# A hand-scheduled attention and state-space kernel: new durations and delays in the planner's model, a new seed and rules, and an earlier release of score banks

## The chip, the cores and the metric

The kernel runs on one core of one Trainium2 chip. The metric is the device time of one execution in microseconds (us), as the median of several. Engines are called by the names of the profile: PE is TensorE (matmuls), DVE is VectorE, ACT is ScalarE, POOL is GpSimd, SP is SyncE, which issues most DMAs.

## The reference, cut to what matters

Two independent layers on sequences of 2048 rows and 640 columns; their outputs stand side by side.

```python
# A: a diagonal state-space layer
Lam_bar = exp(dt * Lam);  B_bar = ((Lam_bar - 1) / Lam)[:, None] * Bmat
Bu = einsum("bld,pd->blp", x + 0j, B_bar)
for t in range(L):
    h = Lam_bar[None, :] * h + Bu[:, t, :]
y = 2.0 * einsum("blp,dp->bld", hseq, Cmat).real + x * Dskip
# B: attention, 32 query heads of width 20, one shared key and value head
q = (x @ wq).reshape(B, S, 32, 20);  k = x @ wk;  v = x @ wv
p = softmax(einsum("bhqd,bkd->bhqk", q, k) * 20 ** -0.5)
o = einsum("bhqk,bkd->bhqd", p, v).reshape(B, S, 640) @ wo
out = concatenate([y, o], axis=-1)
```

## The kernel before, in words

**The work.** The scores are 2048 tiles of 128 keys by 512 queries: 4 blocks of queries, 8 groups of four heads, 16 chunks of keys, 4 heads. A *block* in the code (`b`, 32 of them) is one group of heads for one block of queries, 64 tiles. Each tile needs a score matmul, an exponential, and a product with V.

**Two ways to make an exponential.** Most tiles go to ACT: a *fill* (`fill`, L1482) is one PE step that writes two or three score tiles into the banks of one of two PSUM slots (SC0, SC1, three banks each), and one ACTIVATE (L1519) turns them into probabilities (`PR`), 1024 or 1536 columns wide. The two slots alternate. The other tiles, *D tiles*, go to DVE (`fill_d`, L1717): it evicts the scores as int16 (L864, `BIG<-SC` or `BIG<-MB`), which reads as a piecewise-linear power of two in bfloat16; three shifted copies of that are made by DVE (L864, `BIG<-BIG`, one tile or two at a time) or POOL (L1834, two at a time) in `copy` (L1820), and the four versions are weighted in the product with V. An ACT tile takes one matmul with V (`MB<-PR,VP`), a D tile takes four (`MB<-BIG,VS`). A D tile is often the third tile of a fill, with only the first two going to ACT. `SHARE` limits how many of the tiles are D tiles, `LAST` and `POOL_LAST` how late they and POOL's copies may come.

**PE's two modes.** In *row mode* (S) up to four matmuls of 32 rows each run side by side; the scores use it. In *column mode* (C) four matmuls of 32 columns each do; the products with V and nearly all other products use it. Going from one to the other costs time (`SWITCH` in the planner).

**The other work.** Projections, the state-space layer (units, Y products, scans on DVE) and the output products are tasks with due times counted in score tiles (`background`, `unit_due`, `C_DUE`, `CB_FROM`, `O_STEP`, `Y_STEP`). Their matmuls go in column mode between fills, or as *riders*: `board` (L810) puts one piece of such a product on the row of the array that a fill leaves free. A step may consist of several pieces. The first goes ahead of the score matmuls and the rest behind them; the step then signals twice, once at the last score and once at its end (`op.twice`).

```python
            fns = [self.piece(r, *m, x) for m in step[0]]
            if len(fns) > 1:
                op.twice = len(op.fns)
            op.fns[:] = fns[:1] + op.fns + fns[1:]
```

`keep_source` adds filler matmuls (`MB<-KT,VZ`) when PE had little to do lately.

**What sets the order.** `planned` (L547) runs a simulation of the engines (`Schedule`) when the kernel is built. Each step has a duration, reads and writes; `seen` (L109) says when another engine sees its end, `ready` and `pick` choose the next step of an engine by priority, slack and rules, and `rules` (L1435) changes the rules with the number of tiles done (`STAGES`, L1444). `SEEDS` spreads the due times of tasks at random. `Emitter.plan` (L272) then turns the order into five fixed instruction streams with semaphore waits. On the chip nothing is chosen any more: each engine goes through its stream and waits where it must. A reader of a PSUM bank waits for the last step that wrote to it.

Of the kernel before, what the change touches and what calls it, by code (L numbers as in the profile page):

```python
# [24 lines left out]
class Op:  # L25
# [3 lines left out]
                 "seq", "land", "dma_key", "idx", "tail", "mode", "load", "late", "port", "after", "due", "table", "psum", "twice", "fence", "lands", "clear")  # L29

    def __init__(self, eng, fns, dur, deps=(), prio=5, reads=(), writes=(), prev=None, gate=None, hook=None,
# [7 lines left out]
        self.port, self.after, self.due, self.table, self.twice, self.fence, self.lands = port, [], None, None, None, None, None  # L39
# [6 lines left out]
class Schedule:  # L46
# [10 lines left out]
    SWITCH, STAY = 97.0, 1.2  # L57
# [66 lines left out]
    def ready(self, op):  # L124
# [3 lines left out]
        for d in op.deps:  # L128
            if d.end is None:
                return None  # L130
            v = self.seen(d, op.eng)
            if v > r:
                r = v
        return r

    def begin(self, op, eng):
# [32 lines left out]
        for lag in (0.0, 60.0, 100.0, 110.0, 115.0, 130.0, 150.0, 200.0):  # L169
# [92 lines left out]
class Emitter:  # L262
# [9 lines left out]
    def plan(self):  # L272
# [6 lines left out]
        needed = set()  # L279
        self.streams = {e: [] for e in Schedule.ENGINES}  # L280
        for op in self.order:
# [3 lines left out]
            def dep(o):  # L285
# [5 lines left out]
                if src not in need or need[src].idx < o.idx:  # L291
                    need[src] = o
# [3 lines left out]
            if op.fence is not None:  # L296
                need[e] = op.fence
# [6 lines left out]
            for k in op.reads:  # L304
                w = last_w.get(k)
                dep(w)
# [8 lines left out]
            if op.dma_key is not None:  # L315
                prev = dma_count.get(op.dma_key)
                if prev is not None:
                    need[op.dma_key] = prev[1]
            w = []
            K = know[e]  # L320
            items = sorted(need.items(), key=lambda kv: (kv[0] == e, -kv[1].start))
            for src, o in items:
                if K.get(src, -1) >= o.idx:
                    continue
                w.append(o)
# [3 lines left out]
                if K.get(src, -1) < o.idx:  # L329
                    K[src] = o.idx  # L330
            kept = []
            for o in w:
                src = o.dma_key if o.dma_key is not None else o.eng
                implied = False
                for o2 in w:
                    if o2 is not o and snap[id(o2)].get(src, -1) >= o.idx:
                        implied = True
                if not implied:
                    kept.append(o)
                    needed.add(id(o))  # L340
# [31 lines left out]
    def replay(self, rng):  # L372
# [3 lines left out]
        for op in self.order:  # L376
            e = op.eng
            t = free[e]
            for o in self.waits_of[id(op)]:
                lag = S.OUT["dma"] if o.dma_key is not None else S.OWN.get(e, 0.0) if o.eng == e else S.OUT[o.eng]  # L380
# [15 lines left out]
    def emit(self, block):  # L396
# [70 lines left out]
class Build:  # L467
# [77 lines left out]
    SEEDS, REPLAYS = (10005,), 12  # L545
# [264 lines left out]
    def board(self, op, used):  # L810
# [5 lines left out]
        for r in self.rides:  # L816
# [19 lines left out]
            if len(fns) > 1:  # L836
                op.twice = len(op.fns)
# [423 lines left out]
    def qt_task(self, bank, g=0):  # L1261
# [20 lines left out]
        if g:  # L1282
            ev = self.dve(lambda e: e.tensor_copy(dst, bank.ap), 645, deps=[prev], reads=[bank.key], writes=[key], prio=self.EV)
# [21 lines left out]
    def q_task(self, qb, blk, bank):  # L1305
# [6 lines left out]
        ev = self.dve(lambda e: e.tensor_copy(dst, bank.ap), 645, deps=[prev], reads=[bank.key], writes=[key], prio=self.EV)  # L1312
# [122 lines left out]
    def rules(self):  # L1435

        while self.stages and self.stages[0][0] <= self.tile_n:
# [12 lines left out]
        (250, {'ALONE': 2.237, 'PV': 1.984, 'COPY1': 0.897}),  # L1450
        (500, {'STAY': 1.083, 'SPARE': 86.026, 'SOON': 2941.52, 'ALONE': 2.429, 'TASK': 0.989, 'PV': 1.9, 'P1': 0.519, 'PVEV':
            0.2, 'SCARCE': 7, 'BACKLOG': 7, 'SHARE': 0.301}),
        (850, {'STAY': 1.2, 'dve': 185.73, 'MARGIN': 628.898, 'REFILL': 766.143, 'SPARE': 148.045, 'LAG': 240.378, 'SOON':
            2730.774, 'ALONE': 1.449, 'TASK': 0.95, 'PV': 1.889, 'EV': 0.544, 'P1': 0.5, 'SCARCE': 8, 'BACKLOG': 9}),
        (1200, {'STAY': 0.876, 'MARGIN': 648.138, 'REFILL': 905.623, 'LAG': 190.385, 'ALONE': 2.13, 'PV': 1.718, 'EV': 0.506,
            'COPY': 0.534, 'COPY1': 0.9}),
        (1600, {'STAY': 1.2, 'pe': 196.33, 'EARLIER': 5, 'ALONE': 1.525, 'PV': 1.9, 'COPY': 0.554, 'COPY1': 0.897, 'P1OWN': 0.321,
            'GRACE': 41.523}),
# [23 lines left out]
    def fill(self, op, i):  # L1482
# [28 lines left out]
        for m in extra:  # L1511
# [4 lines left out]
        op.dur = self.mmt(512, n_mm + (len(op.fns) > n_mm))  # L1516
# [3 lines left out]
                      0.8333 * 512 * n + 64, table="exp",  # L1520
# [196 lines left out]
    def fill_d(self, op, m, bank=None):  # L1717
# [12 lines left out]
        first = self.dve(self.ts(self.dr(h.index), bank.ap, 16256.0, 0.0, ALU.add, ALU.max), 645, deps=[op],  # L1730
# [61 lines left out]
    LAST = 16  # L1792
    POOL_LAST = 25
# [13 lines left out]
    POOL2 = 605.0  # L1807
# [43 lines left out]
    def pv_source(self):  # L1851
# [10 lines left out]
        scarce = len(self.d_free()) < self.SCARCE  # L1862
        for j in range(4):
# [752 lines left out]
```

## Time and profile before

| | us |
|---|---|
| runs of the kernel | 701.4, 702.19, 702.4 |
| median | 702.19 |
| the profiled execution | 701.32 |
| its span in the trace | 699.6 |

The profile is one execution. A row of the page gives a line, an engine, an operation, the tiles out<-in, their shape and count, then the busy time, the mean length of one in ns, and the idle time of that engine just before these instructions with what ended most of it. Rows of the timeline give the start, the time to the end of the last, the engine, line and operation, and how many were merged. Rows of windows give for each stretch the busy times of PE, weight loads, DVE, ACT and POOL with their counts, then PE's granted clock, the DMA share and GB/s. The chain of waits follows the work back from the last instruction. PE's granted clock is 1.00 throughout the main part.

### The profile page before, as it was taken

What the parts mean: (1) busy time and instruction counts of PE and PEld (TensorE: products, weight loads), DVE (VectorE), ACT (ScalarE), POOL (GpSimd) and SP (SyncE); (2) the same over time, 40 slices, a digit from 0 to 9 for tenths busy, and PEclk for the clock granted to TensorE, in tenths of its full rate; (3) what the DMA queues carried; (4) which work ended last, traced back from release to release, by engine and by line L of the source; (5) the groups of instructions that cost most, each with busy time, mean ns of one, the idle gap of its engine ahead of it and who ended that gap; (6) DMA issues with size and microseconds to landing.
All of it is one profiled execution on the core that took longest, in us unless ns stands there. A gap on an engine that the chain in (4) does not pass through costs nothing.

```text
span 699.6 us, 27005 instructions
## 1 busy us (share of the span) xinstructions
PE 685.1 (98%) x11348; PEld 248.6 (36%) x11350; DVE 629.7 (90%) x1211; ACT 685.3 (98%) x701; POOL 467.7 (67%) x796
## 2 busy tenths in 40 slices
PE   9999999999999999999999999999999999999997
PEld 5323232334333333534343323334333333343323
DVE  7899999999999987898979997899999999997695
ACT  7999999999999999999999999999999999999996
POOL 4266776443868898464777885777866777768780
PEclk9999999999999999999999999999999999999999
DMA  9649732001111111000040010131000011100001
GB/s 220 170 109 224 177 85 58 28 8 31 28 49 32 28 43 37 23 19 17 17 83 21 15 42 21 35 56 22 12 15 20 12 26 39 29 19 19 27 15 40
DMA packets 77590, 34.46 MB, mean 49 GB/s; under 512 B 58350, under 2 KB 77470, under 8 KB 77470
## 3 DMA queue, kind: packets, MB, share of 16 engines
q1 hardware_dynamic: 76506, 32.44, 19.0%
q8 instruction: 91, 1.49, 0.9%
q10 hardware_dynamic: 964, 0.29, 0.2%
q14 instruction: 29, 0.24, 0.1%
HBM read 11.53 MB, written 9.75 MB: 30 GB/s over the span
## 4 chain that ended last, share of the span: by engine, by line
PE 66%; ACT 33%; DVE 0%; issue 0%; DVEq 0%
ACT PR L1519 33%; PE MB L727 26%; PE MB L797 17%; PE SC L727 14%; PE MB L807 7%; PE SC L1155 1%; PE MB L723 1%; PE SC L723 0%; DVE PR L859 0%; PE MB L1272 0%; DVE mab L1161 0%; DVEq L510 0%; PE SC L1211 0%; DVE pvsb L859 0%; DVE M L863 0%
## 5 line engine op out<-in xcount | busy, mean ns | idle before, releaser
L1519 ACT ACTIVATE PR<-SC 128x1024 bf16<-128x1024 f32 (+1 forms) x677 | 670.3, 1171 | 3.9 <-PE SC L727 2.8
L1834 POOL INT64_ADD BIG<-BIG x761 | 455.4, 614 | 200.6 <-DVE BIG L864 72.3
L864 DVE TENSOR_SCALAR BIG<-SC 128x512 int16<-128x512 f32 x548 | 369.4, 684 | 49.8 <-PE SC L727 43.1
L727 PE MATMUL SC<-QT,KT 32*128 32x512 bf16 x2013 | 264.5, 384 | 6.9 <-ACT PR L1519 5.9
L727 PE MATMUL MB<-BIG,VS 128*32 128x512 bf16 x2332 | 257.4, 383 | 0.4 <-DVE pvsb L1901 0.2
L727 PE MATMUL MB<-PR,VP 128*32 128x512 bf16 x1465 | 213.7, 384 | 0.0
L727 PEld LDWEIGHTS SC<-QT,KT 32*128 32x128 bf16 x2013 | 66.7, 90 | 157.4 <-ACT PR L1519 94.7
L727 PEld LDWEIGHTS MB<-BIG,VS 128*32 128x32 bf16 x2332 | 61.7, 95 | 65.1 <-issue 40.6
L727 PEld LDWEIGHTS MB<-PR,VP 128*32 128x32 bf16 x1465 | 51.4, 94 | 44.6 <-issue 32.8
L797 PE MATMUL MB<-CT,W 128*32 128x320 bf16 (+2 forms) x996 | 52.7, 301 | 0.6 <-issue 0.6
L864 DVE TENSOR_SCALAR BIG<-BIG 128x1024 int16<-128x1024 int16 (+1 forms) x116 | 45.8, 427 | 1.5 <-PE MB L727 1.0
L807 PE MATMUL MB<-xaT,BT 32*128 32x256 bf16 x200 | 38.6, 272 | 0.7 <-ACT PR L1519 0.6
L797 PE MATMUL MB<-CA,W 128*32 128x512 bf16 (+1 forms) x640 | 35.4, 302 | 0.0
L797 PE MATMUL MB<-xaT,BA 128*32 128x256 bf16 x800 | 32.2, 275 | 0.0
L807 PE MATMUL MB<-diagD,xaT 32*128 32x128 bf16 x320 | 31.4, 217 | 0.0
L807 PEld LDWEIGHTS MB<-diagD,xaT 32*128 32x128 bf16 x320 | 17.7, 92 | 28.9 <-ACT PR L1519 20.2
L797 PEld LDWEIGHTS MB<-CT,W 128*32 128x32 bf16 x996 | 22.4, 96 | 15.3 <-issue 7.5
L2086 DVE CAST stg<-MB 128x512 bf16<-128x512 f32 x35 | 23.9, 683 | 1.9 <-PE MB L797 1.8
L797 PE MATMUL MB<-xaT,BT 128*32 128x256 bf16 x600 | 25.1, 274 | 0.0
L859 DVE TENSOR_TENSOR prod<-MB,tab 128x1024 bf16<-128x1024 f32 x20 | 24.3, 1216 | 0.4 <-PE MB L797 0.2
L864 DVE TENSOR_SCALAR BIG<-MB 128x512 int16<-128x512 f32 x35 | 23.8, 679 | 0.0
L2353 DVE TENSOR_TENSOR_SCAN g<-sc,hst,prod 128x256 bf16<-128x256 f32 x30 | 22.8, 772 | 0.1
(174 smaller groups left out, 488.1 us busy)
## 6 DMA issues: line engine op xcount, KB each, us to landing
out_dram<-stg SPq DMA_DIRECT2D x31, 128.0 KB, 1.8
qd<-BIG SPq DMA_DIRECT2D x20, 128.0 KB, 2.5
QT<-qd SPq DMA_DIRECT2D x28, 80.0 KB
OP<-pvsb SPq DMA_DIRECT2D x105, 20.0 KB
rdP<-recs SPq DMA_DIRECT2D x105, 20.0 KB
lbd<-BA SPq DMA_DIRECT2D x5, 320.0 KB, 4.1
CT<-in_B_x_dram SPq DMA_DIRECT2D x2, 640.0 KB, 5.3
BA<-in_A_B_re_dram SPq DMA_DIRECT2D x1, 800.0 KB, 9.4
```

Of the source, the lines that this page charges most:

```text
L723: r = e.matmul(out[32 * j:32 * j + 32], lhsT=lhsT[:, 32 * j:32 * j + 32], rhs=rhs, start=start, stop=stop, tile_position=(0, 32 * j), skip ...
L727: return lambda e: e.matmul(out, lhsT=lhsT, rhs=rhs, start=start, stop=stop, **kw)
L797: x = e.matmul(out[32 * j:32 * j + 32], lhsT=lhsT[:, 32 * j:32 * j + 32], rhs=rhs, start=start, stop=r.end is tag, tile_position=(0, 32 * ...
L807: return lambda e: e.matmul(out, lhsT=lhsT[at], rhs=rhs[at], start=False, stop=r.end is tag, tile_position=(32 * row, 0), skip_group_check ...
L859: return lambda e: e.tensor_tensor(out, a, b, op)
L864: return lambda e: e.tensor_scalar(out, a, s1, s2, op0=op0, op1=op1)
L1155: prev = self.pe([lambda e, x=x, c=c, n=n, at=at: e.matmul(bank.cols(n * x, n * x + n), lhsT=p.wks[:, 128 * c:128 * c + 128], rhs=p.xbT[:, ...
L1519: ex = self.act(lambda e: e.activation(dst, t[:, 0:512 * n], ACT.Exp, scale=1.0 / UNIT), 0.8333 * 512 * n + 64, table="exp", deps=[op], re ...
L1834: op.fns.append(lambda e: e.int64_add(words(dst), words(src), add))
L2086: ev = self.dve(lambda e: e.tensor_copy(st, bank.ap), 645, deps=[prev], reads=[bank.key], writes=[key], prio=self.EV, gate=(lambda: last.e ...
L2353: o = self.dve(lambda e, ri=ri, init=init: e.tensor_tensor_scan(p.g[:, u, ri, :], rdec, p.prod[:, 1, 0, ri, :], init, ALU.mult, ALU.add), ...
```

## The change

Three things are changed together. The edits of the model and of the rules touch only what the planner believes and prefers; the kernel gets other instruction streams through them.

1. *The model.* A change of PE's mode is taken as 105.5 ns and 10 more towards column mode; a change counts as starting when the results that the step reads are seen, not before. The delays between engines are set for each pair. A fill is one pass of 512 columns, whatever is in it. The exponential is 6 ns shorter, the evictions on DVE 7 ns, POOL's copy 18 ns.
2. *The rules.* A new seed, new values in all six stages, and new due times.
3. *The waits.* A reader of a PSUM bank that a step with riders wrote, where the bank is not the rider's own, waits for the step's first signal, that is the last score, and not for its end.

```diff
-    SWITCH, STAY = 97.0, 1.2
+    SWITCH, AFTER, STAY = 105.5, 10.0, 1.2
+    SEEN = {("pe", "act"): 225.0, ("pe", "dve"): 225.0, ("pe", "pool"): 285.0, ("act", "pe"): 92.0, ("dve", "pe"): 0.0, ("pool", "pe"): 0.0,
+            ("dve", "pool"): 170.0}
...
-        return op.end + self.OUT[op.eng]
+        return op.end + self.SEEN.get((op.eng, eng), self.OUT[op.eng])
...
             v = self.seen(d, op.eng)
+            if op.eng == "pe" and op.mode == self.mode and d.eng != "pe" and d.dma_key is None:
+                v += self.SWITCH
...
             if op.mode != self.mode:
-                op.dur += self.SWITCH
+                op.dur += self.SWITCH + (self.AFTER if op.mode == "C" else 0.0)
...
-            def dep(o):
+            def dep(o, key=None):
...
-                if src not in need or need[src].idx < o.idx:
-                    need[src] = o
+                at = o.idx - 0.5 if key is not None and o.twice is not None and key != o.rider else o.idx
+                if src not in need or need[src][0] < at:
+                    need[src] = at, o
...
             for k in op.reads:
-                w = last_w.get(k)
-                dep(w)
+                dep(last_w.get(k), k if k in self.psum else None)
...
+                if at < o.idx:
+                    self.first.add((id(op), id(o)))
...
-                        be.wait_ge(self.sems[o.eng], self.value[id(o)])
+                        be.wait_ge(self.sems[o.eng], self.value[id(o)] - ((id(op), id(o)) in self.first))
...
-    SEEDS, REPLAYS = (10005,), 12
+    SEEDS, REPLAYS = (750698,), 12
...
-                op.twice = len(op.fns)
+                op.twice, op.rider = len(op.fns), r.bank.key
...
     STAGES = (
-        (0, {'STAY': 1.2, 'PAUSE': 500.0, 'pe': 192.807, 'dve': 150.0, 'KEEP_C': 3, 'OPEN': 1, 'PATIENCE': 2500.0, 'MARGIN':
+        (0, {'STAY': 1.452, 'PAUSE': 500.0, 'pe': 192.807, 'dve': 150.0, 'KEEP_C': 3, 'OPEN': 1, 'PATIENCE': 2497.12, 'MARGIN':
...
-            7, 'AHEAD': 10, 'CAP': 3, 'ROOM': 4, 'ALONE': 1.397, 'TASK': 0.95, 'PV': 2.034, 'EV': 0.52, 'P1': 0.5, 'COPY': 0.554,
-            'COPY1': 0.836, 'P1OWN': 0.42, 'PVEV': 0.209, 'SCARCE': 8, 'BACKLOG': 9, 'GRACE': 55.439, 'SHARE': 0.29, 'MISC_FIRST':
+            7, 'AHEAD': 12, 'CAP': 2, 'ROOM': 4, 'ALONE': 1.397, 'TASK': 0.95, 'PV': 2.034, 'EV': 0.511, 'P1': 0.5, 'COPY': 0.554,
+            'COPY1': 0.836, 'P1OWN': 0.42, 'PVEV': 0.2, 'SCARCE': 8, 'BACKLOG': 9, 'GRACE': 55.439, 'SHARE': 0.29, 'MISC_FIRST':
...
-        op.dur = self.mmt(512, n_mm + (len(op.fns) > n_mm))
+        op.dur = self.mmt(512)
...
-                      0.8333 * 512 * n + 64, table="exp",
+                      0.8333 * 512 * n + 58, table="exp",
...
-    LAST = 16
-    POOL_LAST = 25
+    LAST = 8
+    POOL_LAST = 29
...
-    POOL2 = 605.0
+    POOL2 = 587.0
...
+        later = s.SWITCH if s.mode == "C" else 0.0
         for j in range(4):
-            can = [e for e in q[j] if e[4].end is not None and s.seen(e[4], "pe") <= t and self.vp_seen(e[1], t)]
+            can = [e for e in q[j] if e[4].end is not None and s.seen(e[4], "pe") <= t - later and self.vp_seen(e[1], t)]
...
-    C_DUE = 200
-    CB_FROM, CB_STEP = 358.689, 15.665
+    C_DUE = 103.686
+    CB_FROM, CB_STEP = 336.444, 15.665
...
-    Q_FROM, Q_STEP = (0, 30, 110, 190), 10.976
-    O_FROM, O_STEP, O_CLASS = 31.576, 38.293, 1
-    SSM_FROM, SSM_TO, Y_STEP, GRACE = 150.723, 1780, 23.0, 40
+    Q_FROM, Q_STEP = (0, 30, 110, 190), 11.747
+    O_FROM, O_STEP, O_CLASS = 31.576, 43.688, 1
+    SSM_FROM, SSM_TO, Y_STEP, GRACE = 150.723, 1780, 14.199, 40
```

The remaining lines of the diff set the evictions of DVE to 638 ns where they were 645, one product to 1144 for 1135, and the other five stages of the rules.

More of the change, by code (lines that the diff above doesn't have):

```diff
@@ L28 @@
     __slots__ = ("eng", "fns", "dur", "deps", "prio", "reads", "writes", "prev", "gate", "hook", "start", "end",
-                 "seq", "land", "dma_key", "idx", "tail", "mode", "load", "late", "port", "after", "due", "table", "psum", "twice", "fence", "lands", "clear")
+                 "seq", "land", "dma_key", "idx", "tail", "mode", "load", "late", "port", "after", "due", "table", "psum", "twice", "rider", "fence", "lands", "clear")
     def __init__(self, eng, fns, dur, deps=(), prio=5, reads=(), writes=(), prev=None, gate=None, hook=None,
@@ L38, in __init__ @@
         self.mode, self.load, self.late = mode, load, False
-        self.port, self.after, self.due, self.table, self.twice, self.fence, self.lands = port, [], None, None, None, None, None
+        self.port, self.after, self.due, self.table, self.fence, self.lands = port, [], None, None, None, None
+        self.twice = self.rider = None
         self.psum = any(k[0] == "B" and k[1:].isdigit() for k in self.reads)
@@ L168, in begin @@
         self.at(self.free[eng])
-        for lag in (0.0, 60.0, 100.0, 110.0, 115.0, 130.0, 150.0, 200.0):
+        for lag in (0.0, 60.0, 92.0, 100.0, 105.5, 110.0, 115.0, 130.0, 150.0, 170.0, 197.5, 225.0):
             self.at(op.end + lag)
@@ L279, in plan @@
         needed = set()
+        self.first = set()
         self.streams = {e: [] for e in Schedule.ENGINES}
@@ L296, in plan @@
             if op.fence is not None:
-                need[e] = op.fence
+                need[e] = op.fence.idx, op.fence
             for k in op.writes:
@@ L328, in plan @@
                         K[s2] = v
-                if K.get(src, -1) < o.idx:
-                    K[src] = o.idx
+                if K.get(src, -1) < at:
+                    K[src] = at
             kept = []
[L332 to L340, printed above, removed]
+            for src, at, o in w:
+                if any(o2 is not o and snap[id(o2)].get(src, -1) >= at for _, _, o2 in w):
+                    continue
+                kept.append(o)
+                needed.add(id(o))
+                if at < o.idx:
+                    self.first.add((id(op), id(o)))
             waits_of[id(op)] = kept
@@ L1450 @@
[L1450 to L1456, printed above, removed]
@@ L1874, in pv_source @@
         prio = 0.9 if tight or complete else self.PV
-        return Op("pe", [], self.mmt(512, len(group)), prio=prio, mode="C", load=128.0 * len(group), hook=lambda op: self.pv(op, b, group))
+        return Op("pe", [], self.mmt(512), prio=prio, mode="C", load=128.0 * len(group), hook=lambda op: self.pv(op, b, group))
     def vp_seen(self, kc, t):
```

39 lines of the change are left out of this document (25 added, 14 removed).

## The prediction

> **What bounds the kernel now.** I read the shares of busy time first, then the costliest groups split by shape, then who waited for whom.
>
> ```profile
> span 699.6 us, 27005 instructions
> PE 685.1 (98%) x11348; PEld 248.6 (36%) x11350; DVE 629.7 (90%) x1211; ACT 685.3 (98%) x701; POOL 467.7 (67%) x796
> L1519 ACT ACTIVATE PR<-SC 128x1024 bf16<-128x1024 f32 (+1 forms) x677 | 670.3, 1171 | 3.9 <-PE SC L727 2.8
> ```
> ```profile
> L1519 ACT ACTIVATE PR<-SC 128x1024 bf16<-128x1024 f32 x566 | 532.6, 1100 | 3.9 <-PE SC L727 2.8 <-PE MB L727 0.5
> L1519 ACT ACTIVATE PR<-SC 128x1536 bf16<-128x1536 f32 x111 | 159.9, 1534 | 0.0
> ```
> ```profile
> 200.00:300.00 100.00, 98.94 (x1767) 35.44 (x1759) 88.01 (x160) 100.00 (x104) 74.70 (x126) 1.00 0.14 33
> 400.00:500.00 100.00, 99.83 (x1759) 36.55 (x1753) 92.00 (x162) 100.00 (x103) 73.62 (x124) 1.00 0.15 32
> ```
>
> PE and ACT both show 98%, but they are not equal. The 677 exponentials keep ACT busy for 670.3 us without a break, and in front of all of them together ACT is idle for only 3.9 us. In the windows from 200 and from 400 us it is busy for 100.00 of 100 us (fourth of the five busy times, behind PE, weight loads and DVE). The ends of the matmuls are modelled by the profiler, so PE's share hides slack. ACT is the bound, and 3.9 us is all that a better order can take out of the middle of the kernel.
>
> What does one exponential cost in a full row of them? The starts and the ends give two answers, so I look at a place where a start came late.
>
> ```profile
> 479.39 2.54 ACT L1519 ACTIVATE PR<-SC 128x1536 bf16<-128x1536 f32 x2
> 482.54 1.23 ACT L1519 ACTIVATE PR<-SC 128x1024 bf16<-128x1024 f32 x1
> 483.60 1.08 ACT L1519 ACTIVATE PR<-SC 128x1024 bf16<-128x1024 f32 x1
> 481.64 3.04 ACT L1519 ACTIVATE PR<-SC 128x1024 bf16<-128x1024 f32 x3
> ```
>
> Each row is start, length, count. The starts here go 481.64, 482.54, 483.60: 0.90 us apart, then 1.06. The ends go from 479.39+2.54 = 481.93 to 481.64+3.04 = 484.68, which is 2.75 us for three, or 0.917 each, with no gap where the start was late; the instruction just shrank from 1.23 to 1.08 us. So starts may run ahead, but ACT delivers one 1024-wide exponential per **0.917 us**. For the 1536-wide ones there is a full row of them from 130 to 149 us:
>
> ```profile
> 130.59 1.54 ACT L1519 ACTIVATE PR<-SC 128x1536 bf16<-128x1536 f32 x1
> 147.03 1.72 ACT L1519 ACTIVATE PR<-SC 128x1536 bf16<-128x1536 f32 x1
> L1519 ACT ACTIVATE PR<-SC 128x1536 bf16<-128x1536 f32 x12 | 16.6, 1640 | 0.0
> L1519 ACT ACTIVATE PR<-SC 128x1024 bf16<-128x1024 f32 x3 | 3.2, 1135 | 0.0
> ```
>
> The last two rows count the window from 130.6 to 148.3. From the end of the first (132.13) to the end of the last (148.75) eleven wide ones and two of the narrow ones end (the third began before the first row): (16.62 - 2 x 0.917)/11 = **1.344 us**. The length grows from 1.54 to 1.72 as the starts run ahead. Check: 566 x 0.917 + 111 x 1.344 = 668.2 against 670.3 busy.
>
> **The change part by part.** The new order, counted instruction by instruction against the old, has: exponentials of two tiles 566 -> 565, of three tiles 111 -> 116; tiles whose exponential VectorE makes 583 -> 570; their copies on DVE 111 -> 57 pairs and 5 -> 2 singles, on POOL 761 -> 797 pairs; matmuls with V 3797 -> 3758; the 256-column filler matmuls 228 -> 188; changes of PE between row mode and column mode 1336 -> 1355.
>
> *1. Thirteen tiles move to ACT.* 5 x 1.344 - 1 x 0.917 = **+5.8 us** on the engine that bounds. Nothing covers it: ACT has 3.9 us idle in all, so at least 5.8 - 3.9 = 1.9 us must show; with no idle taken back, 5.8.
>
> [...]
>
> *2. PE gets lighter.* The chain of waits gives its prices:
>
> ```profile
> 305.99 0.33 PE SC L727 x3
> 306.32 0.55 PE MB L727 x8
> 306.86 0.32 PE SC L727 x3
> 307.19 0.55 PE MB L797 x16
> 303.49 0.76 PE MB L797 x12
> ```
>
> A fill (three score matmuls side by side) and the change to column mode take 0.32. Two groups of four 512-column matmuls and the change back take 0.55, three take 0.76: 0.21 to 0.22 for a group, 0.11 for a change, and 0.11 for a group of 256 columns (x16 is four of these). The 39 fewer V matmuls are 10 groups (-2.1 us), the fillers 10 short groups (-1.1), 6 fewer row-mode steps -1.3, other products that now ride in fills -1.2, 19 more changes of mode +2.1: **-3.6 us of PE work**, off the bounding path except where PE was late.
>
> These places are what ACT's idle time consists of. A fill with two groups is 0.32 + 0.55 = 0.87 us, under the 0.917 of an exponential; with three it is 1.08, over it. So an order is late where it puts three or more groups between fills for longer than ACT's lead covers. I took both orders in stretches of fills, with these prices for PE and 0.917 or 1.344 for ACT, and added up only what PE needs above ACT. Stretches of 12 give 5.1 us for the old order and 2.8 for the new, stretches of 14 give 4.2 and 1.8; these are the lengths at which the old order comes out near its traced 3.9. The new sums are half of the old, so I take 3.9 -> 1.9: **-2.0 us**. Bounds: -3.9 (no idle left) and 0 (new stalls replace the old).
>
> *3. Readers of score banks wait for one increment less.* Both orders have 192 row-mode steps with rider pieces behind the scores. In the new one 188 ACT and 159 DVE waits stop at the scores.
>
> ```profile
> 585.04 0.39 PE L727 MATMUL SC<-QT,KT 32*128 32x512 bf16 x3
> 585.48 1.02 ACT L1519 ACTIVATE PR<-SC 128x1024 bf16<-128x1024 f32 x1 [0.59 <-PE SC L727]
> 530.99 0.39 PE L727 MATMUL SC<-QT,KT 32*128 32x512 bf16 x3
> 531.05 0.33 PE L807 MATMUL MB<-diagD,xaT 32*128 32x128 bf16 x3
> 531.48 1.02 ACT L1519 ACTIVATE PR<-SC 128x1024 bf16<-128x1024 f32 x1 [0.24 <-PE SC L727]
> ```
>
> Both exponentials found ACT empty. Without riders ACT began 0.44 us after the scores, with three small ones 0.49. So 0.05 us is gained, but only where ACT is waiting; elsewhere it goes into the lead of the starts. If it came at all 188 waits it would be 9 us, more than all of ACT's idle time, so it cannot. If half of the new order's 1.9 us sits behind riders in gaps of some 0.2 us, it is five to ten places: **-0.3 us**, bounds 0 and -0.5. PE itself does the same work, and the second increment was there before.
>
> *4. VectorE and GpSimd.*
>
> ```profile
> L864 DVE TENSOR_SCALAR BIG<-SC 128x512 int16<-128x512 f32 x548 | 369.4, 684 | 49.8 <-PE SC L727 43.1 <-PE MB L727 0.8
> L864 DVE TENSOR_SCALAR BIG<-BIG 128x1024 int16<-128x1024 int16 x111 | 44.8, 434 | 1.5 <-PE MB L727 1.0
> L1834 POOL INT64_ADD BIG<-BIG x761 | 455.4, 614 | 200.6 <-DVE BIG L864 72.3 <-PE SC L727 23.5 <-PE MB L727 16.7
> ```
>
> DVE loses 13 x 0.68 + 54 x 0.43 = 32 us, POOL gains 36 x 0.61 = 22 us under its 200.6 us of idle time. Neither ends a wait of ACT for long (the exponentials' idle time is put down to PE), so **0**. If the cover goes, a fill waits for a late eviction; DVE, 90% busy before, has more room after. The planner keeps the copies of DVE and POOL apart in time, and there POOL's gain is smaller than DVE's loss.
>
> *5. Head and tail.*
>
> ```profile
> 18.48 1.94 ACT PR L1519 x2
> 687.86 1.01 PE MB L723 x64
> 689.19 2.54 PE MB L727 x44
> 685.77 5.51 ACT L1519 ACTIVATE PR<-SC 128x1536 bf16<-128x1536 f32 x4
> ```
>
> Before the first exponential at 18.48 two projection steps, 0.22 us each like a group, move from ahead of the second set of transposes to behind it, on a PE that has warm-up matmuls to give up: 0, bounds -0.3 and +0.4. After the last fill the old order has 12 V groups in 2.54 us; the new has three groups of 16 narrow matmuls (0.25 each, from x64 in 1.01) and 8 V groups, 2.5 us: **-0.1**, bounds -0.4 and +0.4. DMA issues change place on SP's queue (transposed loads of B and C earlier against stores), with the same counts; no row shows an exponential waiting for SP, so 0.
>
> **Sum:** +5.8 - 2.0 - 0.3 - 0.1 = **+3.4 us**. The profiled execution (701.32 us, of which the span is 699.6) would be 704.7; it lies 0.9 below the median of the runs shown, so the median goes from 702.19 to **705.6 us**.
>
> **Rivals.** *A, the new order starves ACT nowhere.* For it: over stretches of 32 fills or more PE's sum hardly ever exceeds ACT's. Against: the short stretches do. +5.8 - 3.9 - 0.1 = +1.8, 704.0 us; down to +1.0 if the 0.1 us that each restart of ACT costs (1.02 against 0.917) is counted as idle too.
>
> *B, the idle time stays,* because new stalls come that no price shows.
>
> ```profile
> 620.22 0.24 PE L797 MATMUL MB<-CT,W 128*32 128x128 bf16 x3 [0.57 <-issue]
> ```
>
> Here PE stopped for 0.57 us with nothing to wait for. For it: some of these happen in any order. Against: one such row in the windows I opened. +5.8 - 0.1 = +5.7, 707.9 us; a few more would make 709.
>
> *C, faster: ACT's pace is that of the starts,* some 0.903 and 1.330 (the 13 starts from 130.59 to 147.03 take 16.44 us). ACT's work is then 659.0 before and 664.7 after. The last start lies 1.33 x 3 behind 685.77, at 689.76, 671.3 behind the first, so the old order has 13.7 us of stall; cutting that as stretches of 16 fills do at this pace (7.3 -> 2.7) leaves 5.0: +5.7 - 8.7 = -3.0 and **699.2 us**. It decides once the stalls fall below 13.7 - 5.7 = 8.0. Against it stand the ends above, 0.917 apart through a late start. [...]
>
> *D, the change does not do what it says:* the early release finds nobody waiting. That only drops the -0.3: 705.9 us.
>
> **How the numbers follow.** Forecast with D 0.57 (704.6 to 706.8), A 0.15, B 0.22, C 0.06. The range **702.9 to 708.3** takes in A to its lower bound and most of B, and leaves out C and B's end. A change under 0.2% (1.4 us, 700.8 to 703.6) can't be told from none: faster 0.06 (C), same 0.13 (the low half of A, a weak C), slower 0.81.
>
> **What would show it.** Right: 681 exponentials busy for about 676 us, idle before them near 2 us, ends 0.917 apart; first exponential at 18.5 +/- 0.3; exponentials with an empty ACT 0.44 us after the scores with and without riders. Wrong: ends closer than 0.917 in full rows (C), idle time at 4 us or above (B), or a first exponential or a tail off by over 0.5 us.

## The result and the profile after

The changed kernel took 706.99 us (median of 11 runs, 705.46 to 707.38) and the kernel before, on the same chip, 702.22 us: a ratio of 1.0057, 95% interval 1.0043 to 1.0072, or +4.8 us where +3.4 was forecast. In the profiled executions the span went from 699.6 to 705.6 us.

The first fence is from the page of the changed kernel: the span, the shares of busy time and the group of all exponentials. The second splits that group by shape, and the third has two windows of 100 us (busy times in the order PE, weight loads, DVE, ACT, POOL, then granted clock, DMA share and GB/s).

```profile
span 705.6 us, 26827 instructions
PE 688.5 (98%) x11273; PEld 248.2 (35%) x11273; DVE 611.8 (87%) x1141; ACT 690.1 (98%) x705; POOL 490.6 (70%) x832
L1527 ACT ACTIVATE PR<-SC 128x1024 bf16<-128x1024 f32 (+1 forms) x681 | 675.4, 1213 | 4.0 <-PE SC L731 3.6
```
```profile
L1527 ACT ACTIVATE PR<-SC 128x1024 bf16<-128x1024 f32 x565 | 532.2, 1137 | 3.5 <-PE SC L731 3.0 <-PE SC L801 0.2
L1527 ACT ACTIVATE PR<-SC 128x1536 bf16<-128x1536 f32 x116 | 167.8, 1583 | 0.6 <-PE SC L731 0.6
```
```profile
200.00:300.00 100.00, 98.94 (x1718) 35.77 (x1714) 87.18 (x155) 99.82 (x103) 76.19 (x128) 1.00 0.14 34
400.00:500.00 100.00, 99.28 (x1620) 34.40 (x1617) 91.10 (x159) 99.99 (x104) 76.69 (x128) 1.00 0.13 32
```

ACT still bounds. Its exponentials are busy 5.1 us longer (670.3 before), and the idle time in front of them has not moved: 3.9 before, 4.0 after. So the tiles that went to ACT show in full, and the 2.0 us of idle time that lighter work on PE was to save did not come.

Adding up by the ends of the exponentials makes this sharper. The steps between ends are 0.917 and 1.343 us in both traces (0.9167 and 1.3433 unrounded). With these the exponentials take 667.95 us before and 673.75 after; whatever lies between two ends beyond that is idle time of ACT.

```
us                     before   after   difference
first exponential       18.48   19.23     +0.75
work of exponentials   667.95  673.75     +5.80
first one, extra length  0.11    0.11      0.00
idle time, by ends       4.75    4.11     -0.64
last end to span's end   8.30    8.42     +0.12
sum                                       +6.03   (spans: 699.58 and 705.61)
```

The first exponential of each trace lasts 1.02 us, 0.11 more than a step. Counted this way the old order's idle time is 4.75 us, where the prediction took 3.9 from the rows.

The idle time has another make-up than before. Before, one stop of PE "with nothing to wait for" was seen, at 620 us, and the rest was nearly all PE's work between fills. The timeline of the changed kernel from 361 us (start, length, engine, line, operation, count, and in brackets the idle time before it):

```profile
361.87 0.23 PE L801 MATMUL MB<-CT,W 128*32 128x128 bf16 x4
361.93 0.22 PE L801 MATMUL MB<-BIG,xaT 128*32 128x128 bf16 x2
363.18 0.29 PE L801 MATMUL MB<-BIG,xaT 128*32 128x128 bf16 x6 [1.03 <-issue]
363.42 0.39 PE L731 MATMUL SC<-QT,KT 32*128 32x512 bf16 x3
363.86 1.02 ACT L1527 ACTIVATE PR<-SC 128x1024 bf16<-128x1024 f32 x1 [0.93 <-PE SC L731]
```

PE stands for a good microsecond between the second and the third of eight matmuls of one piece, which wait for nothing: 1.03 us idle by the row, 1.25 from one start to the next. The next fill is late by that, and ACT idles 0.93 us (1.04 by ends). Three such stops and a small one (286.65, 363.18, 501.82 and 627.02 us) make 2.1 of the 4.1 us. Two waits early on, one for a copy of POOL (0.60) and one for DVE (0.35), make another 1.0; they are absent in a second profile of the same kernel. PE's own work between fills leaves some 1.1 us.

### The profile page after: what moved, and what is told of

It reads as the page before. It is cut to its first block, busy times and chain, and to the rows that moved or that the text cites. A ratio compares the mean times of both kernels' runs of the same rounds, so it can differ in the third digit from the quotient of the medians.

```text
span 705.6 us, 26827 instructions
## 1 busy us (share of the span) xinstructions
PE 688.5 (98%) x11273; PEld 248.2 (35%) x11273; DVE 611.8 (87%) x1141; ACT 690.1 (98%) x705; POOL 490.6 (70%) x832
## 4 chain that ended last, share of the span: by engine, by line
PE 50%; ACT 47%; DVE 1%; issue 1%; DMA 0%; POOL 0%; DVEq 0%
ACT PR L1527 47%; PE MB L731 19%; PE MB L801 12%; PE SC L731 10%; PE MB L811 6%; PE SC L1159 1%; PE MB L727 1%; PE SC L727 0%; PE SC L801 0%; DMA qd<-BIG 0%; DVE BIG L868 0%; PE SC L811 0%; DVE PR L863 0%; DVE prod L863 0%; PE MB L1276 0%
## 5 line engine op out<-in xcount | busy, mean ns | idle before, releaser
L1842 POOL INT64_ADD BIG<-BIG x797 | 478.3, 618 | 181.8 <-DVE BIG L868 53.9
L811 PE MATMUL MB<-xaT,BT 32*128 32x256 bf16 x184 | 35.5, 272 | 0.5 <-ACT PR L1527 0.2
L811 PE MATMUL MB<-diagD,xaT 32*128 32x128 bf16 x320 | 31.3, 216 | 0.1
L811 PEld LDWEIGHTS MB<-diagD,xaT 32*128 32x128 bf16 x320 | 17.7, 92 | 29.9 <-ACT PR L1527 21.5
L801 PE MATMUL MB<-xaT,BT 128*32 128x256 bf16 x616 | 27.4, 274 | 0.0
L868 DVE TENSOR_SCALAR BIG<-BIG 128x1024 int16<-128x1024 int16 (+1 forms) x59 | 23.6, 432 | 0.7 <-POOL BIG L1842 0.5
L801 PE MATMUL MB<-WO,OP 128*32 128x512 bf16 (+1 forms) x428 | 22.0, 304 | 0.0
```

What stands on the lines that cost most here:

```text
L801: x = e.matmul(out[32 * j:32 * j + 32], lhsT=lhsT[:, 32 * j:32 * j + 32], rhs=rhs, start=start, stop=r.end is tag, tile_position=(0, 32 * ...
L811: return lambda e: e.matmul(out, lhsT=lhsT[at], rhs=rhs[at], start=False, stop=r.end is tag, tile_position=(32 * row, 0), skip_group_check ...
L868: return lambda e: e.tensor_scalar(out, a, s1, s2, op0=op0, op1=op1)
L1842: op.fns.append(lambda e: e.int64_add(words(dst), words(src), add))
```

## The experiments

**The early release alone, and everything but it.** The first kernel is the old one with only the third part of the change; the second is the new one with the old waits.

```diff
# e1: the kernel before
-                        be.wait_ge(self.sems[o.eng], self.value[id(o)])
+                        be.wait_ge(self.sems[o.eng], self.value[id(o)] - ((id(op), id(o)) in self.first))
...
# e2: the new kernel
-                at = o.idx - 0.5 if key is not None and o.twice is not None and key != o.rider else o.idx
+                at = o.idx
```

> The instruction order of before, instruction for instruction; only the readers of score banks stop waiting at the last score (345 waits). ACT theory (the time is the sum of the exponentials at 0.917 and 1.344 us, plus ACT's idle time, plus head and tail): the release helps only where ACT is idle and the fill has rider pieces, so -0.3 us against before (0 to -0.5). Rival (readers gain everywhere): -5 us or more. An exponential that finds ACT empty starts 0.44 us after the scores, with riders too.

> The instruction order of the changed kernel; only the waits are those of before. ACT theory: +0.3 us against the changed kernel (0 to +0.5), so some 707.2 us. Rival (the early release is what costs the 4.8 us, because ACT or DVE now gets in the way of the riders on PE): back to about 702. It is also a second profile of the same order: the places where PE stops inside long runs of 128-column matmuls without a wait (0.3 to 1.2 us each, four of them) come back if the run causes them, and are elsewhere if they are chance.

Measured: 702.64 us for the release alone, 0.9997 of the kernel before (0.9977 to 1.0018), and 707.01 us for all but the release, 1.0055 (1.0033 to 1.0076). The exponentials on the pages of the first and of the second:

```profile
L1519 ACT ACTIVATE PR<-SC 128x1024 bf16<-128x1024 f32 (+1 forms) x677 | 670.6, 1169 | 4.6 <-PE SC L727 3.5
```
```profile
L1527 ACT ACTIVATE PR<-SC 128x1024 bf16<-128x1024 f32 (+1 forms) x681 | 675.6, 1207 | 5.4 <-PE SC L731 4.5
```

The release is worth nothing that can be measured, either way; the 0.3 us that was forecast is smaller than these intervals. In the second kernel PE's stops come back where they were in the new one (285.60, 362.91, 503.00 and 627.96 us), so they belong to the order and are not chance. That the release works can still be read. ACT stood empty behind a fill with riders (the two L811 rows), first in the new kernel and then, at the same place, with the old waits:

```profile
627.24 0.39 PE L731 MATMUL SC<-QT,KT 32*128 32x512 bf16 x3
627.24 0.22 PE L811 MATMUL MB<-BIG,xaT 32*128 32x128 bf16 x1
627.31 0.21 PE L811 MATMUL MB<-BIG,xaT 32*128 32x128 bf16 x1
627.68 1.45 ACT L1527 ACTIVATE PR<-SC 128x1536 bf16<-128x1536 f32 x1 [0.57 <-PE SC L731]
```
```profile
628.18 0.39 PE L731 MATMUL SC<-QT,KT 32*128 32x512 bf16 x3
628.66 1.45 ACT L1527 ACTIVATE PR<-SC 128x1536 bf16<-128x1536 f32 x1 [0.33 <-PE SC L731]
```

In the new kernel it began 0.44 us after the scores, as one without riders does; with the old waits it took 0.48. That is 0.04 us, and it counts only where ACT stands empty.

**Model and rules apart.** The third kernel has the new model, delays and waits with the old seed, rules and due times; the fourth the reverse.

```diff
# e3: the new kernel with the old rules (all STAGES and due times)
-    SEEDS, REPLAYS = (750698,), 12
+    SEEDS, REPLAYS = (10005,), 12
...
# e4: the kernel before with the new rules (all STAGES and due times)
-    SEEDS, REPLAYS = (10005,), 12
+    SEEDS, REPLAYS = (750698,), 12
```

> The new durations, delays and waits, with the seed, stages and due times of before. Its order has 539 exponentials of two tiles and 137 of three: 678.4 us of ACT against 668.2 before, and PE has 9.5 us of work after its last fill against 6.4. ACT theory: +10.2 us and up to +3 for the longer tail, 712 to 716 us. Rival (the new rules, not the model, cost the time): 701 to 704.

> The old durations, delays and waits, with the seed, stages and due times of the change. Its order has 563 exponentials of two tiles and 114 of three: 669.5 us of ACT, +1.3 against before, and 9.9 us of PE work after the last fill against 6.4. ACT theory: +1.3 and up to +3.5 for the tail, 703.5 to 707 us. Rival (the rules cost what the change costs, whatever ACT's sum is): 707 or more with ACT's idle time up by 3 us or more.

Measured: 713.23 us, ratio 1.0139 (1.0097 to 1.0181), and 710.67 us, ratio 1.0113 (1.0070 to 1.0156). The first was expected (712 to 716), the second was not: 703.5 to 707 had been forecast for it, with ACT's idle time unchanged. By shape, first the new model, then the new rules:

```profile
L1523 ACT ACTIVATE PR<-SC 128x1024 bf16<-128x1024 f32 x539 | 508.3, 1149 | 3.7 <-PE SC L731 3.5
L1523 ACT ACTIVATE PR<-SC 128x1536 bf16<-128x1536 f32 x137 | 196.2, 1622 | 0.9 <-PE MB L731 0.9
```
```profile
L1523 ACT ACTIVATE PR<-SC 128x1024 bf16<-128x1024 f32 x563 | 530.5, 1097 | 8.6 <-PE SC L727 6.8 <-PE MB L727 0.8
L1523 ACT ACTIVATE PR<-SC 128x1536 bf16<-128x1536 f32 x114 | 164.8, 1534 | 0.2 <-PE SC L727 0.2
```

With the old rules the new model hands ACT 539 x 0.917 + 137 x 1.343 = 678 us, 10 us more than the kernel before, and leaves it idle 4.1 us by ends, for 4.75. With the old model the new rules hand it under 2 us more but starve it for some 11 us by ends; some 3.2 us of these are PE's stops without a wait, of the kind looked at below. What follows the last exponential takes 11.1 us for 8.3. The profiled execution (713.08 us) was the slowest of its four, 2.4 us above the median, so the 11 are more than the usual execution has. Neither half pays; together they lose least. It is the model that moves tiles to ACT.

**Is it ACT's price in the model?** The model has the exponential at 0.903 us, the step between *starts*; the ends are 0.917 apart. One entry was set to the ends, then also another seed tried.

```diff
# e7 and e8: the new kernel
-    EARLIER = {"dve": 40.0, "act": 8.0}
+    EARLIER = {"dve": 40.0, "act": 0.0}
...
-                      0.8333 * 512 * n + 58, table="exp",
+                      0.8333 * 512 * n + 63.5, table="exp",
...
# e8 also
-    SEEDS, REPLAYS = (750698,), 12
+    SEEDS, REPLAYS = (962839,), 12
```

> The new kernel with one entry of its model changed: the exponential costs what its ends show (0.917 and 1.344 us; the new model has 0.903 and 1.330), seed and rules stay. The order that comes of it has 574 and 106 exponentials where the new one has 565 and 116, so ACT's work is 668.8 us against 674.0 (-5.2). Theory that tiles went to ACT because the model holds it to be quicker than it is: about 676 - 5 = 671 us busy, and by the stretches of 12 and 14 fills 2.6 us more of PE's lateness, and 8.6 us of PE work behind the last fill for 6.8 (+1.8): -0.8, so 706.2 us. If idle time that no such sum shows comes on top, as with the old model under the new rules (+4 there): 708 to 710 us. If ACT's work were not what counts: 709 us or above with ACT's busy time near 671.

> As the kernel with the changed price of the exponential, with another seed for the due times: 571 and 108 exponentials (668.7 us, -5.3 against the new kernel), lateness of PE by the stretches of 12 and 14 fills 2.3 us more than in the new one, PE work behind the last fill 7.2 us for 6.8. Sum -2.6: 704.4 us, above the kernel before still. If idle time that no sum shows comes on top: 706 to 708 us.

Measured: 705.27 us, ratio 1.0055 (1.0043 to 1.0067), and 704.96 us, ratio 1.0051 (1.0039 to 1.0063), beside 701.49 of the kernel before in the same session. The exponentials of the first:

```profile
L1527 ACT ACTIVATE PR<-SC 128x1024 bf16<-128x1024 f32 (+1 forms) x680 | 671.8, 1159 | 4.5 <-PE SC L731 2.4
```

The price does move the tiles: 574 and 106 exponentials, 5.2 us less of ACT's work. More than half of it is given back: idle time by ends is 6.2 us for 4.1, and the span ends 9.2 us behind the last exponential for 8.4. Another 0.6 us lies outside the traced span (705.22 us against a span of 702.8, where the other kernels differ by 1.7 to 1.8); no trace shows its cause. Both ratios stay inside the interval of the changed kernel's. So correcting this price brings no gain that can be measured: what ACT is relieved of, PE is in good part late with, and neither order beats the old one.

**What stops PE? Half the instructions in the same time.** All four stops of the new kernel lie inside runs of 128-column matmuls. This kernel keeps the order and PE's time but issues two of the four column tiles in these products; it leaves out half of them.

```diff
# e5: the new kernel, in the function that cuts a product into four column tiles
-            for j in cols:
+            for j in list(cols)[:2] if rhs.shape[-1] == 128 else cols:
```

> The new order, unchanged step by step, but each product that is cut into 128-column matmuls in column mode issues only two of its four column tiles, so half of these products is left out and PE's time for them stays, with half of its instructions. Theory: PE's stops without a wait inside these runs (286, 363, 502 and 628 us in the new kernel, 2.1 us of ACT's idle time by its ends) come of the many short instructions there. Then they are gone, ACT's idle time falls from 4.1 to about 2 us and the time from 707.0 to about 705 us. Rival: the stops have another cause (the place in the program, a transfer): they recur within 1 us of the same places and the time stays at 707 us, idle time at 4 us or more.

Measured: 704.17 us, ratio 1.0036 (1.0024 to 1.0048), beside 1.0060 (1.0046 to 1.0073) when the changed kernel was run again. Its exponentials, and PE at the place of the large stop:

```profile
L1527 ACT ACTIVATE PR<-SC 128x1024 bf16<-128x1024 f32 x565 | 531.9, 1151 | 1.6 <-PE SC L731 1.4
L1527 ACT ACTIVATE PR<-SC 128x1536 bf16<-128x1536 f32 x116 | 168.2, 1593 | 0.0
```
```profile
360.71 0.28 PE L801 MATMUL MB<-BIG,xaT 128*32 128x128 bf16 x4
361.47 0.39 PE L801 MATMUL MB<-BIG,xaT 128*32 128x128 bf16 x8
```

PE stays at 688 us busy, no row of narrow matmuls has a stop, and ACT's idle time by ends falls to 0.85 us. So the stops hang on the number of instructions in a given time (half of the work of these products is gone too, but not PE's time for it). The 0.85 us are about what PE's own lateness costs in the new order.

**Where exactly? PE's instructions come in packets.** The list of DMA queues on the page of the changed kernel, and the DMA view of the microsecond from 360.8:

```profile
q1 hardware_dynamic: 76506, 32.44, 19.7%
q8 instruction: 90, 1.47, 0.9%
```
```profile
q1 hardware_dynamic: 272, 0.07, 237.0%
q8 instruction: 1, 0.02, 6.0%
```

Columns: packets, MB, share of 16 engines (summed over packets that overlap, so it can exceed 100%). Queue q8 moved 90 packets of 16,384 bytes. PE's rows in the trace (matmuls, weight loads, semaphores) number 23,155, or 257 for each packet. That a packet holds 256 is taken from the stops: in the changed kernel they lie 11, 19 and 17 times 256 rows apart. Numbering PE's rows and taking the packets' times from the trace:

```
kernel   PE row  mod 256  packet before    256 rows    PE     resumes after
                          start   took     used in   stopped  packet's end
before   20671    191     617.69  1.26      3.04      0.79       1.27
after     8641    193     283.78  1.39      3.17      0.56       1.48
after    11457    193     360.82  0.95      2.83      1.25       1.41
after    16321    193     499.61  0.95      2.92      0.24       1.27
after    20673    193     624.84  0.93      2.84      0.89       1.25
e3        8641    193     290.06  1.40      2.97      0.87       1.34
e4       16065    193     489.97  1.17      2.80      1.94       1.47
e9       11455    191     357.82  1.63      3.74      1.70       1.24
```

Every stop of over 0.45 us without a wait, 22 of them in thirteen traces, falls on the same row of a packet (191 where a few rows are missing in the trace: that of the kernel before has 11,348 matmuls for 11,350 weight loads), and PE goes on 1.24 to 1.59 us after the packet has ended. A packet of 256 lasts 7.8 us on the average; in a run of 128-column matmuls, with one weight load each, it can be used up in under 3.2. The next may then be late, and whether it is depends on the transfer. Between 20 and 690 us of the thirteen traces 40 packets were used up in 3.2 us or less. In 21 cases PE stopped for over 0.45 us without a wait, in 2 with one, and in 17 for 0.32 us or less or not at all. Three pieces decide: the time from the packet's edge to the start of the next packet's transfer (0.3 to 2.1 us), the transfer itself (0.9 to 1.5), and some 1.35 us until PE goes on. In all 40 cases what their sum has above the time in which the packet was used up gives the stop to within 0.25 us. In the kernel with half of the narrow matmuls no packet is used up in under 3.9 us, and there is no stop.

The first of the three pieces is long where the DMA engines are busy. Windows of 1 us from the edge, in the changed kernel, ahead of its largest stop and of the one at 627 us; the DMA share is the last number but one:

```profile
359.10:360.10 1.00, 1.00 (x62) 0.79 (x51) 0.60 (x3) 1.00 (x3) 1.00 (x3) 1.00 0.99 213
623.29:624.29 1.00, 1.00 (x61) 0.79 (x51) 0.80 (x2) 1.00 (x3) 1.00 (x2) 1.00 0.09 21
```

The six largest of the 40 stops (1.25 to 1.96 us) have a share of 0.63 or more there and 1.7 us or more to the start of the transfer; the other 34 have a share under 0.2. In the few us before each of the six, transposed loads of the state-space input were issued; in the DMA view of the changed kernel from 355 to 360.8 us (count, us to landing):

```profile
xaT<-in_A_x_dram SPq DMA_TRANSPOSE x2, 4.8
```

The test moves the packets without leaving anything out: fillers do their 256 columns as two matmuls of 128, 18 of them (+144 PE instructions), or two (+16).

```diff
# e9 (18 fillers) and e10 (2 fillers): the new kernel
+        fns[0].halves = [self.mm(bank.tensor[32 * j:32 * j + 32, bank.off + a:bank.off + a + 128], p.VZ[:], p.KT[:, a:a + 128], False,
+                                 False, tile_position=(0, 32 * j), skip_group_check=True) for a in (0, 128) for j in range(4)]
         self.n_keep += 1
...
+            for op in [o for o in em.order if o.fns and hasattr(o.fns[0], "halves")][:18]:
+                op.fns[:] = op.fns[0].halves
             em.plan()
```

> The new kernel, nothing left out, but the first 18 fillers (39 to 113 us) do their 256 columns as two matmuls of 128: 72 matmuls and 72 weight loads more, the same columns. Theory: PE's instructions come in 16 KB packets of the instruction queue, 256 of them each (in every trace so far the stops without a wait fall on a PE instruction whose number is 193 modulo 256), and PE stops where it uses up a packet in less than the some 3.5 us that the next one takes. 144 more instructions move these points: by the traced times no packet is then used up in under 3.5 us near 286 and 363 us, and the two that are left lack 0.2 us near 502 and 0.5 us near 624. So the stops of 286 and 363 us are gone, those near 502 and 624 come earlier in the program, again on 193 modulo 256, ACT's idle time by its ends falls from 4.1 to about 2.7 us, and the time is 1.4 us below the new kernel's on the same chip. Rival: the stops belong to their places in the program: they recur before the same matmuls, and the time stays.

> As the kernel with 144 more PE instructions, but only the first two fillers are split: 16 more. By the theory of the packets the four stops stay, each 16 instructions earlier in the program and again on 193 modulo 256, and the time stays within 0.5 us of the new kernel's. If it was the split fillers that helped and not the number of instructions, some of the gain is here too.

> The new kernel unchanged, for the two kernels with moved packets to be compared with on one chip: 1.0057 of the kernel before, stops near 286, 363, 502 and 627 us on 193 modulo 256, the third the smallest.

Measured: 705.68 us, ratio 1.0055 (1.0042 to 1.0067), with 144 more; 705.15 us, 1.0052 (1.0038 to 1.0067), with 16 more; 706.39 us, 1.0060 (1.0046 to 1.0073), unchanged. The exponentials in this order, one fence each:

```profile
L1531 ACT ACTIVATE PR<-SC 128x1024 bf16<-128x1024 f32 (+1 forms) x681 | 674.7, 1221 | 3.0 <-PE SC L733 2.8
```
```profile
L1531 ACT ACTIVATE PR<-SC 128x1024 bf16<-128x1024 f32 (+1 forms) x681 | 675.6, 1210 | 4.7 <-PE SC L733 4.0
```
```profile
L1527 ACT ACTIVATE PR<-SC 128x1024 bf16<-128x1024 f32 (+1 forms) x681 | 675.2, 1212 | 3.9 <-PE SC L731 3.7
```

By ends ACT is idle for 2.4, 5.0 and 3.8 us. In the places the theory holds: with 144 more the stops near 286 and 627 us are gone and the one near 502 is small; with 16 more the first three stay, on the same row of their packets, and the fourth shrinks to nothing. The theory missed the large one. In the kernel with 144 more:

```profile
358.99 0.23 PE L803 MATMUL MB<-CA,W 128*32 128x128 bf16 x2
360.69 0.23 PE L803 MATMUL MB<-CA,W 128*32 128x128 bf16 x2 [1.47 <-issue]
```

The stop did move, to an earlier product (`CA,W` instead of `BIG,xaT`) and again on a packet's edge. But its packet was used up in 3.74 us, more than the 3.5 allowed for, and PE still stopped for 1.70: there the new packet takes 5.4 us from edge to edge. Its transfer started 2.57 us behind the edge, and over that time the DMA share was 0.84. That the transposed loads delay the instruction packet fits all these cases, but no run moves the loads, so it is likely and not shown. In time the three kernels are not told apart: 0.7 us less was measured where 1.4 had been forecast, and the control with 16 more, forecast within 0.5 us, came out 1.2 us *below* the unchanged kernel. The profile with 5.0 us of idle time is of the slowest of its five executions (707.43 us), 2.3 us above their median. What stands is the place of the stops, and the kernel without them.

**Is ACT's pace that of its starts? And what if PE is never late?** The last kernel takes 256 of 512 columns in nearly all products with V, so nearly half of these are left out.

```diff
# e6: the new kernel
+            w = 512 if first else 256
-            op.fns.append(self.mm(bank.tensor[32 * j:32 * j + 32, bank.off:bank.off + 512], lhs, rhs,
+            op.fns.append(self.mm(bank.tensor[32 * j:32 * j + 32, bank.off:bank.off + w], lhs, rhs[:, 0:w],
```

> The new order, but of the products with V all but the first of each block and head take 256 of the 512 columns, so nearly half of that product is left out, and PE is hardly ever late by its own work. Theory that ACT delivers one per 0.917 and 1.344 us (565 and 116 of them, 674 us): only the 1.1 to 1.5 us of idle time go that come from PE's work between fills, and some 0.5 us of the V products behind the last fill; the stops inside runs of narrow matmuls and the waits for DVE and POOL stay: 704.5 to 706 us. Rival, the pace of the starts (0.903 and 1.330): ACT's work is 664.7 us and the time falls to 696 or 697 us.

Measured: 706.65 us, ratio 1.0079 (1.0063 to 1.0095): no faster, with PE at 88%, and above the 706 that was expected at most. Its exponentials, and two pairs of windows:

```profile
L1527 ACT ACTIVATE PR<-SC 128x1024 bf16<-128x1024 f32 (+1 forms) x681 | 674.5, 1292 | 4.1 <-PE SC L731 4.1
```
```profile
360.00:364.00 4.00, 2.48 (x105) 1.62 (x92) 1.73 (x3) 2.55 (x4) 2.35 (x5) 1.00 0.11 24
364.00:368.00 4.00, 3.98 (x66) 1.78 (x63) 2.31 (x4) 3.81 (x4) 2.83 (x5) 0.58 0.06 19
```
```profile
70.00:72.00 2.00, 1.27 (x19) 0.56 (x20) 1.92 (x7) 2.00 (x3) 0.00 (x0) 0.77 1.23 258
72.00:74.00 2.00, 2.00 (x18) 0.60 (x11) 1.45 (x3) 2.00 (x3) 0.88 (x2) 0.50 1.03 297
```

All but six of the 680 steps between ends are 0.917 or 1.343 us to within 0.06, though PE had so much less to do: this is ACT's pace, and nothing faster was waiting behind PE. The six hold 3.2 us. One is the packet's edge at 363 us (1.56), the only one of the four stops that was left; at the other three places PE stood for 0.32 us or less. In the window from 364 PE's granted clock is 0.58 and two more fills are late (0.64). The last large one, 0.91 at 75 us, also lies in a stretch of low clock: PE is busy for 1.27 of the 2 us from 70, and from 72 to 74 the clock is 0.50. The mean clock is 0.985 to 0.994 in all six executions of this kernel, and 0.997 to 1.00 in the eleven of the changed one. PE less busy did not always come with a low clock: in the changed kernel PE is busy for 1.37 of the 2 us from 70, and the clock stays at 1.00 there and in the next two. What lowered it no run shows.

## Why the prediction came out as it did

The forecast was 705.6 us and the time 706.99, inside the range and slower, as forecast. The main term held. Behind the second, two errors partly cancel, which is luck: PE's own lateness fell by some 3 us and not by 2, and PE's stops, which the forecast put at nothing, took much of that back. Two of the prediction's own signs of being wrong came up: idle time at 4 us (4.0 on the page), and a first exponential off by over 0.5 us (0.75). Point by point:

- *Step 1, thirteen tiles to ACT (+5.8): right.* 565 and 116 exponentials ended 0.917 and 1.343 us apart; the work of ACT rose by 5.80 us. The kernel with half of the V products, in which PE is busy 88% and the ends keep this distance, shows that the pace is ACT's own. Rival C fell with that.
- *Step 2, PE lighter (-2.0): the term was mis-sized, by what it left out.* PE's lateness between fills did fall, and by more than was forecast: from some 4.1 to 0.9 to 1.1 us, where 1.9 was said. But the step took ACT's idle time for PE's *work* alone. PE's stops at the edges of its instruction packets were one row in the old trace (0.64 us of ACT's idle time) and are 2.1 us in the new profile, 2.7 in its second. Two waits for POOL and DVE add 1.0 in the first profile. So the idle time went from 4.75 to 4.1 or 3.8 and not to 1.9, and the term of -2.0 measures -0.6 to -1.0. This is rival B's mechanism; "some of these happen in any order" was right, and its 707.9 lies nearer to the time than the forecast does.
- *Step 3, early release (-0.3): nothing measurable.* The mechanism is there, 0.04 us at a waiting ACT in the one place compared, at too few places.
- *Step 4, DVE and POOL (0): right.* DVE lost 18 us of busy time (32 had been worked out; its instructions' lengths add up to 28.5 less, and busy time counts those that overlap once) and POOL gained 23 (22); no wait of ACT behind them recurs in the second profile.
- *Step 5, head (0) and tail (-0.1): tail right, head open within its scatter.* The tail took +0.12. The first exponential at 19.23 us was 0.75 later than before, beyond the bound of 0.4. But the same head of the new order gave 18.41 to 19.29 us over seven profiles, and the old order, with only its waits changed, 19.32. So 18.48 may well have been an early one, and the profile overstates the change: +6.0 in spans against +4.8 in medians.

Rival A fell with the stops: without them the kernel with half of the narrow matmuls, at 0.85 us of idle time, took 2.7 us more than the kernel before, where A had +1.8. Rival D was right in substance. The sum in the end: +5.8 - 0.6 (or -1.0) + 0.1, some +5, against the +4.8 of the medians.

## What to carry to other kernels

Count where an engine's idle time comes from before crediting it to a cause: less work on PE buys only the part that its work had caused. Where products are cut into many narrow matmuls, count PE's instructions as well as its columns: here 40 runs used up 256 of them in 3.2 us or less, in 21 of them PE stopped for over 0.45 us without a wait, and the longest of these stops (1.25 to 1.96 us) came where DMA transfers crowded the engines (a share of 0.63 or more). And take an engine's pace from its ends: the model fed with the starts (0.903 us, where the ends are 0.917 apart) gave the engine that already bounds 5.2 us more work than with the ends. Mending that price moved the work back and brought no gain that could be measured: PE was in good part late with it.

## What the runs showed of the chip

- *Instruction packets.* PE's instructions are loaded while the kernel runs, 256 in a packet of 16 KB. PE stopped at the packet's edge, for up to 1.96 us, where a run of narrow matmuls used one up before the next was there, and went on 1.24 to 1.59 us after the next packet's transfer had ended. Of 40 packets used up in 3.2 us or less, 17 brought no stop over 0.32 us; there the transfer had started 0.3 to 1.0 us behind the edge, and ahead of the seven largest stops 1.7 to 2.6. With half of the narrow matmuls left out, and PE's time the same, all these stops were gone.
- *The clock after a stop.* After stops of 1.74, 1.77 and 1.96 us (the kernels with half of the V products, with 16 more and with the old waits) the granted clock stood at 0.58, 0.62 and 0.59 over some 4 us behind them; after others of 1.70, 1.80 and 1.94 us it did not fall. The first kind, in the kernel with 16 more PE instructions:

```profile
360.00:364.00 4.00, 2.45 (x70) 1.14 (x66) 1.38 (x2) 2.57 (x4) 2.27 (x5) 0.96 0.07 18
364.00:368.00 4.00, 4.00 (x62) 1.57 (x55) 2.04 (x3) 2.80 (x3) 2.14 (x4) 0.62 0.03 7
```

In the changed kernel run again PE was busy for 2.42 us of the same four, no more than here, and the clock stayed at 1.00 in both windows. The lowest clock in the windows shown is the 0.50 from 72 to 74 us in the kernel with half of the V products. Why it fell after some stops and not after others of like length no run shows.
